# A windowed-attention and adapter kernel: fixed engine order, heads paired (n, n+4), fp32 hardware-queue loads, casts on GpSimd

## Chip, cores, metric

The kernel runs on one core of one Trainium2 chip. The metric is the device time of one execution in microseconds (us). Every run comes with a state: "slow" when it is over 1.5% above the fastest run of the same kernel. Ratios are the mean time of one kernel's fast runs over the mean of the other's fast runs of the same rounds on the same chip, so they are not quite the ratio of the medians quoted beside them.

Engines are named as in the profile: PE (matrix multiply), PEld (its weight loads), DVE (VectorE), ACT (ScalarE), POOL (GpSimd), SP (SyncE, which only issues transfers).

## The reference

```python
# q, k, v: (8 batches, 8 heads, 576 positions, 64), fp32
scores = q @ k.T / 8, masked to |i - j| <= 32; attn = softmax(scores); y = attn @ v
x = y as (8 * 576, 512)                      # all heads of a position side by side
logits = x @ w_gate                          # 8 experts, the best 2 are kept, softmax over these 2
out = x + sum over the 2 of weight * (x @ A[e]) @ B[e]     # A: 512 x 16, B: 16 x 512
```

## The kernel before

The work is cut into 32 units, each one pair of heads of one batch (four units a batch). A unit has nine blocks of 64 keys. Scores are made in tiles of eight blocks. The pieces:

```python
def load(b, w):                               # q or k: cast to fp16 during the transfer, issued by POOL
    for g in range(3): nc.gpsimd.dma_start(out=d[:, g]..., in_=src[g])
def load_v(b):                                # 16 small transfers a batch, also from POOL
    ...
def pair_heads(b, w):                         # DVE regroups q or k, 3 copies of 96x1024
    for g in range(3): nc.vector.tensor_copy(...)

def transposes(u, which):                     # tp: 6 PE transposes, then the copies to qT or kT
    ...
    if which == 0: nc.vector.tensor_copy(out=qTs[u % NQ]..., in_=tp...)
    else:          nc.vector.tensor_copy(out=kTs[u % NQ][0:64]...)      # half of kT by DVE
                   nc.scalar.copy(out=kTs[u % NQ][64:128]...)           # half by ACT
def score(t):                                 # ps: mask product, 8 score products, then exp on ACT
    ...
def pv(u):                                    # po: 13 products with v, then the softmax division:
    ...
    nc.vector.reciprocal(out=rc, in_=pog[:, :, :, D])
    nc.vector.tensor_tensor(out=xs[b]..., in0=pog[:, :, :, 0:D], in1=bcast(rc, 3, D), op=ALU.mult)
# ... moe_xT (tx), moe_zl (pz and the gate on DVE, then zs), moe_zT (tz), moe_out (pd), cut ...

for u in range(NU):                           # the loop (loads and pair_heads cut)
    if u + 2 < NU:
        transposes(u + 2, 0); transposes(u + 2, 1)
    if u + 1 < NU:
        scores_through(u + 1)                 # all tiles up to the end of unit u + 1
    pv(u)
    if u >= NP: moe_step(u - NP)              # a quarter of the adapter part of the batch before
```

In this kernel the source order is only a proposal: a scheduler reorders the instructions of each engine when it builds the program.

The softmax here doesn't subtract the row's maximum and nothing guards it: scores larger than these inputs give would overflow.

Of the kernel before, what the change touches and what calls it, by code (L numbers as in the profile page):

```python
# [28 lines left out]
def kernel(  # L29
# [27 lines left out]
    const = tc.alloc_tile_pool(name="const", bufs=1)  # L57
    load_pool = tc.alloc_tile_pool(name="load", bufs=2)
    cast_pool = tc.alloc_tile_pool(name="cast", bufs=2)
    x_pool = tc.alloc_tile_pool(name="xsb", bufs=2)  # L60
    moe_pool = tc.alloc_tile_pool(name="moe", bufs=2)
    ob_pool = tc.alloc_tile_pool(name="ob", bufs=3)
    small = tc.alloc_tile_pool(name="small", bufs=3)
    pw = tc.alloc_tile_pool(name="pw", bufs=3, space=bass.MemoryType.PSUM)
    pt = tc.alloc_tile_pool(name="pt", bufs=2, space=bass.MemoryType.PSUM)


    NV = 3
    vbd = [const.tile([128, NP, NB, 2 * VD], F16, name=f"vbd{i}") for i in range(NV)]

    def load(b, w):
        d = load_pool.tile([96, 3, H, 2, D], F16, tag=f"l{w}", name=f"l{w}")
        src = (q, k)[w][b].rearrange("h (g p j) d -> g p h (j d)", g=3, j=2)
        for g in range(3):
            nc.gpsimd.dma_start(
                out=d[:, g].rearrange("p h j d -> p h (j d)"), in_=src[g])
        raw[b, w] = d

    def load_v(b):
        d = vbd[b % NV]  # L80
        src = v[b].rearrange("(n h) (a p j) d -> h j n p a d", h=2, p=32, j=2)
        for n in range(NP):
            for h in range(2):
                for j in range(2):
                    p0 = 64 * h + 32 * j
                    nc.gpsimd.dma_start(  # L86
                        out=d[p0:p0 + 32, n, :, VD * h:VD * h + D], in_=src[h, j, n])

    def pair_heads(b, w):
        d = cast_pool.tile([96, 3, 2, H, D], F16, tag=f"c{w}", name=f"c{w}")  # L90
        for g in range(3):
            nc.vector.tensor_copy(out=d[:, g],
                                  in_=raw[b, w][:, g].rearrange("p h j d -> p j h d"))
        qk[b, w] = d

    raw, qk = {}, {}
    load(0, 0)
    load(0, 1)

    ident = const.tile([128, 128], F16)  # L100
    make_identity(nc, ident)

    for i in range(NV):
        nc.vector.memset(vbd[i], 0.0)
        nc.vector.memset(vbd[i][0:64, :, :, D], 1.0)
        nc.vector.memset(vbd[i][64:128, :, :, VD + D], 1.0)

    load_v(0)
    pair_heads(0, 0)
    pair_heads(0, 1)  # L110


    mask = const.tile([128, 4, 128], F16)
    nc.gpsimd.memset(mask, 0.0)
    for s in range(4):
        jk = s % 2
        blk = mask[32 * s:32 * s + 32]
        nc.gpsimd.affine_select(out=blk, in_=blk, compare_op=ALU.is_ge, fill=NEG,
                                base=-jk, channel_multiplier=-2,
                                pattern=[[0, 4], [1, 128]])  # L120
        nc.gpsimd.affine_select(out=blk, in_=blk, compare_op=ALU.is_ge, fill=NEG,  # L121
                                base=64 + jk, channel_multiplier=2,
                                pattern=[[0, 4], [-1, 128]])

    NQ = 4
    qTs = [const.tile([128, 2, 320], F16, name=f"qT{i}") for i in range(NQ)]
    kTs = [const.tile([128, NB, 128], F16, name=f"kT{i}") for i in range(NQ)]
    for t in qTs:
        nc.vector.memset(t[:, :, 0:16], 0.0)
        nc.vector.memset(t[:, :, 304:320], 0.0)  # L130
    for t in kTs:
        nc.vector.memset(t, 0.0)
    NPT = 4
    PTs = [const.tile([128, TB, 256], F16, name=f"PT{i}") for i in range(NPT)]
    for t in PTs:
        nc.vector.memset(t, 0.0)

    load(1, 0)
    load(1, 1)
    load_v(1)  # L140

    WA_sb = const.tile([128, 4, ER + E], F16)
    for c in range(4):
        nc.gpsimd.dma_start(
            out=WA_sb[:, c, 0:ER],
            in_=moe_A.transpose([1, 0, 2])[128 * c:128 * c + 128],
        )
    nc.gpsimd.dma_start(
        out=WA_sb[:, :, ER:],
        in_=moe_w_gate.rearrange("(c p) e -> p c e", p=128),  # L150
    )
    B_sb = const.tile([128, DD], F16)
    nc.gpsimd.dma_start(out=B_sb, in_=moe_B.rearrange("e r d -> (e r) d"))


    def transposes(u, which):
        b, n = divmod(u, NP)
        src = qk[b, which].rearrange("p g j h d -> p g j (h d)")
        tp = pt.tile([128, 1024], F16, tag="t", name="tp")
        for g in range(3):  # L160
            for j in range(2):
                if which == 0:
                    o = tp[:, 288 * j + 96 * g:288 * j + 96 * g + 96]
                else:
                    o = tp[:, 192 * g:192 * g + 192].rearrange(
                        "p (a j k) -> p a j k", a=3, j=2)[:, :, j]
                nc.tensor.matmul(  # L167
                    out=o, lhsT=src[:, g, j, 128 * n:128 * n + 128],
                    rhs=ident[0:96, 0:96], is_transpose=True, start=True, stop=True)
        if which == 0:  # L170
            nc.vector.tensor_copy(
                out=qTs[u % NQ][:, :, 16:304],
                in_=tp[:, 0:S].rearrange("p (j s) -> p j s", j=2))
        else:
            kt = tp[:, 0:S].rearrange("p (a k) -> p a k", k=64)
            nc.vector.tensor_copy(out=kTs[u % NQ][0:64, :, 0:64], in_=kt[0:64])  # L176
            nc.scalar.copy(out=kTs[u % NQ][64:128, :, 64:128], in_=kt[64:128])  # L177

# [17 lines left out]
    def pv(u):  # L196
# [4 lines left out]
        for g in range(NG):  # L201
# [11 lines left out]
        rc = small.tile([128, NG, 2], F32, tag="rc", name="rc")  # L213
        nc.vector.reciprocal(out=rc, in_=pog[:, :, :, D])  # L214
        nc.vector.tensor_tensor(  # L215
            out=xs[b][:, :, 128 * n:128 * n + 128].rearrange("p g (h d) -> p g h d", h=2),
            in0=pog[:, :, :, 0:D], in1=bcast(rc, 3, D), op=ALU.mult)


# [13 lines left out]
    def moe_zl(b):  # L233
        xT = st[b, "xT"]
        pz = pw.tile([128, 1024], F32, tag="w", name="pz")
        for g in range(NG):
            for c in range(4):
                nc.tensor.matmul(out=pz[:, GS * g:GS * g + ER + E],  # L238
                                 lhsT=xT[:, g, c, :], rhs=WA_sb[:, c, :],
                                 start=(c == 0), stop=(c == 3))  # L240
        pzg = pz[:, 0:GS * NG].rearrange("p (g c) -> p g c", c=GS)
        lg = pzg[:, :, ER:ER + E]

        def sm(name, shape):
            return small.tile([128, NG] + shape, F32, tag=name, name=name)
        m1, m2, dm, s = sm("m1", []), sm("m2", []), sm("dm", []), sm("s", [])
        is1, lm, is2, gate = sm("is1", [E]), sm("lm", [E]), sm("is2", [E]), sm("gate", [E])
        nc.vector.tensor_reduce(out=m1, in_=lg, axis=AX.X, op=ALU.max)
        nc.vector.tensor_tensor(out=is1, in0=lg, in1=bcast(m1, 2, E), op=ALU.is_ge)
        nc.vector.scalar_tensor_tensor(out=lm, in0=is1, scalar=-1e30, in1=lg,  # L250
                                       op0=ALU.mult, op1=ALU.add)
        nc.vector.tensor_reduce(out=m2, in_=lm, axis=AX.X, op=ALU.max)
        nc.vector.tensor_tensor(out=dm, in0=m2, in1=m1, op=ALU.subtract)
        nc.scalar.activation(out=dm, in_=dm, func=AF.Exp)
        nc.vector.tensor_tensor(out=is2, in0=lm, in1=bcast(m2, 2, E), op=ALU.is_ge)
        nc.vector.tensor_scalar(out=s, in0=dm, scalar1=1.0, scalar2=None, op0=ALU.add)
        nc.vector.reciprocal(out=s, in_=s)
        nc.vector.tensor_tensor(out=is2, in0=is2, in1=bcast(dm, 2, E), op=ALU.mult)
# [31 lines left out]
            r0 = S * b + 128 * g - 32  # L290
            nc.sync.dma_start(out=out[r0 + lo:r0 + hi], in_=ob[lo:hi, i])

    def moe_step(m):
        b, s = divmod(m, NP)
        if s == 0:
            for g in range(NG):
                moe_xT(b, g)
            moe_zl(b)
        elif s == 1:
            moe_zT(b)  # L300
            moe_out(b, [0, 1])
        elif s == 2:
            moe_out(b, [2, 3])
        else:
            moe_out(b, [4])


    for w in (0, 1):
        transposes(0, w)
    for w in (0, 1):  # L310
        transposes(1, w)
    t_done = 0

    def scores_through(u):
        nonlocal t_done
        last = min(NT - 1, (NB * u + NB - 1) // TB)
        while t_done <= last:
            score(t_done)
            t_done += 1

    scores_through(0)
    for u in range(NU):
        b, n = divmod(u, NP)
        if n == 0 and b + 1 < B:
            pair_heads(b + 1, 0)
        if n == 1 and b + 1 < B:
            pair_heads(b + 1, 1)
        if n == 0 and b + 2 < B:
            load(b + 2, 0)
            load(b + 2, 1)  # L330
            load_v(b + 2)
        if u + 2 < NU:
            transposes(u + 2, 0)
            transposes(u + 2, 1)
        if u + 1 < NU:
            scores_through(u + 1)
        pv(u)
        if u >= NP:
            moe_step(u - NP)
    for m in range(NU - NP, NU):  # L340
        moe_step(m)

    for p in (pt, pw, small, ob_pool, moe_pool, x_pool, cast_pool, load_pool, const):
        p.release()
# [30 lines left out]
```

## Time and profile before

| | before |
|---|---|
| time, median (range) | 216.44 us (215.23 to 217.51, 4 runs) |
| span of the profiled run | 211.4 us |
| fourth softmax division starts (batch 0 through the attention) | 44.4 us |
| from there to the last division, per batch (7 batches) | 21.35 us |
| last division to the end | 17.55 us |

The last three rows are read from the starts of the 32 reciprocals on DVE: 44.37 us for the fourth and 193.85 us for the last, (193.85 - 44.37) / 7 = 21.35.

The page of the profile: busy time of each engine with its share of the span; then, of the lines that cut the span into 40 slices, PEclk, the granted PE clock in tenths; then the chain of work that ended last, by engine.

```profile
PE 147.6 (70%) x1600; PEld 114.4 (54%) x1600; DVE 119.9 (57%) x337; ACT 85.6 (40%) x109; POOL 128.3 (61%) x197
...
PEclk9999999999969995999699997999999999999955
...
PE 52%; DVE 19%; POOL 11%; ACT 9%; issue 4%; DMA 3%; ACTq 0%; POOLq 0%
```

No engine is full. PE leads the chain, so what PE waits for counts. The view of waits for PE (waiting line, releaser, us in total, times, longest):

```profile
PE tz L271 <- DVE zs L262: 21.0, 8, 3.3
PE ps L182 <- POOL mask L121: 12.0, 1, 12.0
PE tp L167 <- POOL ident masks.py:199: 9.7, 1, 9.7
PE tx L227 <- DVE xT L230: 4.8, 6, 1.3
...
PE ps L186 <- ACT kT_164 L177: 2.4, 3, 1.3
```

PE stands still once per batch for the gate (zs), 21.0 us in all. Three windows round one gate wait (window, length, busy us and counts of PE, PEld, DVE, ACT, POOL; then granted clock, DMA share, GB/s):

```profile
98.00:101.90 3.90, 1.00 (x15) 0.75 (x13) 3.48 (x14) 1.75 (x3) 3.90 (x6) 1.00 0.73 46
102.20:106.20 4.00, 3.66 (x24) 1.97 (x22) 0.91 (x2) 1.76 (x3) 4.00 (x7) 0.57 1.03 75
106.80:112.00 5.20, 5.20 (x60) 4.25 (x57) 1.86 (x4) 3.90 (x5) 3.62 (x7) 1.00 1.46 177
```

Over the 4 us after the idle stretch the granted clock averages 0.57, so this PE wait is paid for twice.

### The profile page before, as it was taken

How to read it: one execution, taken by the hardware profiler on the slowest of the kernel's cores; microseconds unless marked ns; L12 is line 12 of the kernel's file. 1: busy time of each engine (PE TensorE's matmuls, PEld its weight loads, DVE VectorE, ACT ScalarE, POOL GpSimd, SP SyncE). 2: the span in 40 equal slices, each digit the busy share in tenths (PEclk: the TensorE clock that was granted, in tenths of full speed). 3: DMA queues.
4: the chain of work that ended last, by engine and by line, in shares of the span. 5: the costliest groups of instructions: out<-in, count | busy, mean ns of one | idle time of the engine just before them, and what ended most of it. 6: DMA issues, size and time to landing. Idle time of an engine off the chain costs nothing.

```text
span 211.4 us, 4124 instructions
## 1 busy us (share of the span) xinstructions
PE 147.6 (70%) x1600; PEld 114.4 (54%) x1600; DVE 119.9 (57%) x337; ACT 85.6 (40%) x109; POOL 128.3 (61%) x197
## 2 busy tenths in 40 slices
PE   0030279998299949987699729964998599848481
PEld 0010158996268835876378626864687468726330
DVE  6787026668814891379346851688349734844700
ACT  2001015663357334553275144723683466246032
POOL 7999995999799469835983797699480000000000
PEclk9999999999969995999699997999999999999955
DMA  6998099999999998998999999999993023003306
GB/s 59 157 63 56 1 140 125 67 42 154 138 101 144 244 96 54 208 210 87 63 167 249 103 89 153 258 98 147 172 189 55 0 90 136 5 0 123 100 0 223
DMA packets 86642, 24.12 MB, mean 114 GB/s; under 512 B 81888, under 2 KB 82016, under 8 KB 86624
## 3 DMA queue, kind: packets, MB, share of 16 engines
q0 software_dynamic: 81376, 14.44, 86.3%
q1 hardware_dynamic: 5248, 9.44, 13.2%
q8 instruction: 12, 0.20, 0.4%
q14 instruction: 6, 0.05, 0.1%
HBM read 28.85 MB, written 9.44 MB: 181 GB/s over the span
## 4 chain that ended last, share of the span: by engine, by line
PE 52%; DVE 19%; POOL 11%; ACT 9%; issue 4%; DMA 3%; ACTq 0%; POOLq 0%
PE ps L186 13%; PE po L206 9%; PE ps L182 7%; PE pd L282 5%; PE tp L167 5%; PE pd L284 5%; POOL vbd_82 L86 4%; DVE xb L215 4%; PE pz L238 3%; DMA l_189<-in_k_dram 3%; DVE zs L262 3%; PE tx L227 3%; DVE xT L230 3%; ACT zT L274 3%; PE tz L271 2%
## 5 line engine op out<-in xcount | busy, mean ns | idle before, releaser
L86 POOL DMA_DIRECT2D vbd_83<-in_v_dram x48 | 29.3, 616 | 12.0 <-DMA vbd_83<-in_v_dram 4.8
L86 POOL DMA_DIRECT2D vbd_82<-in_v_dram x48 | 29.3, 617 | 9.0 <-DMA l_496<-in_q_dram 2.7
L182 PE MATMUL ps<-mask,ident 128*128 128x512 f16 x72 | 24.6, 423 | 12.7 <-POOL mask L121 12.0
L214 DVE RECIPROCAL rc<-po 128x10 f32<-128x10 f32 x32 | 7.0, 218 | 38.2 <-PE po L206 38.1
L287 ACT COPY obt<-pd 128x1024 f32<-128x1024 f32 (+1 forms) x24 | 20.8, 869 | 16.8 <-PE pd L284 16.0
L215 DVE TENSOR_TENSOR xb<-po,rc 128x640 f16<-128x640 f32 x32 | 26.2, 820 | 0.7
L86 POOL DMA_DIRECT2D vbd_84<-in_v_dram x32 | 19.5, 619 | 7.3 <-DMA vbd_84<-in_v_dram 2.6
L282 PE MATMUL pd<-B_sb,zT 128*128 128x512 f16 x40 | 18.3, 459 | 4.2 <-ACT zT L274 4.2
L271 PE MATMUL tz<-ident,zs 128*128 128x128 f16 x40 | 4.0, 234 | 21.0 <-DVE zs L262 21.0
L227 PE MATMUL tx<-ident,xb 128*128 128x128 f16 x160 | 14.7, 220 | 5.4 <-DVE xT L230 4.8
L284 PE MATMUL pd<-xb,ident 128*128 128x512 f16 x40 | 18.4, 461 | 0.0
L230 DVE COPY xT<-tx 128x512 f16<-128x512 f16 x40 | 15.6, 416 | 2.4 <-PE tx L227 1.6
L177 ACT COPY kT_164<-tp 64x576 f16<-64x576 f16 x8 | 5.1, 633 | 25.0 <-DVE kT_164 L176 25.0
L227 PEld LDWEIGHTS <-xb 128*128 128x128 f16 x160 | 11.3, 101 | 6.9 <-issue 4.9
L271 PEld LDWEIGHTS <-zs 128*128 128x128 f16 x40 | 2.4, 102 | 22.8 <-DVE zs L262 22.8
L182 PEld LDWEIGHTS <-ident 128*128 128x128 f16 x72 | 6.6, 110 | 14.3 <-issue 14.1
L238 PE MATMUL pz<-WA_sb,xT 128*128 128x136 f16 x160 | 13.9, 223 | 0.4 <-DVE xT L230 0.4
L186 PE MATMUL ps<-qT_160,kT_164 128*128 128x128 f16 x72 | 11.1, 317 | 2.4 <-ACT kT_164 L177 2.4
L177 ACT COPY kT_161<-tp 64x576 f16<-64x576 f16 x8 | 5.1, 634 | 18.2 <-DVE kT_161 L176 18.1
L274 ACT COPY zT<-tz 128x640 f16<-128x640 f16 x8 | 5.5, 692 | 16.6 <-PE tz L271 16.6
L191 ACT ACTIVATE PT_178<-ps 128x1024 f16<-128x1024 f32 x9 | 9.2, 1023 | 6.6 <-PE ps L186 5.7
L191 ACT ACTIVATE PT_180<-ps 128x1024 f16<-128x1024 f32 x9 | 9.2, 1023 | 6.1 <-PE ps L186 5.2
(209 smaller groups left out, 375.4 us busy)
## 6 DMA issues: line engine op xcount, KB each, us to landing
out_dram<-obt SPq DMA_DIRECT2D x24, 256.0 KB, 4.0
out_dram<-obt SPq DMA_DIRECT2D x16, 192.0 KB, 2.7
vbd_82<-in_v_dram POOLq DMA_DIRECT2D x48, 36.0 KB, 2.8
vbd_83<-in_v_dram POOLq DMA_DIRECT2D x48, 36.0 KB, 3.4
vbd_84<-in_v_dram POOLq DMA_DIRECT2D x32, 36.0 KB, 3.2
l_85<-in_q_dram POOLq DMA_DIRECT2D x3, 192.0 KB, 4.8
l_89<-in_k_dram POOLq DMA_DIRECT2D x3, 192.0 KB, 6.4
l_185<-in_q_dram POOLq DMA_DIRECT2D x3, 192.0 KB, 4.6
```

The lines of the kernel that those rows point to most:

```text
L86: nc.gpsimd.dma_start(out=d[p0:p0 + 32, n, :, VD * h:VD * h + D], in_=src[h, j, n])
L182: nc.tensor.matmul(out=ps[:, i:i + 4], lhsT=ident, rhs=mask, start=True, stop=False)
L186: nc.tensor.matmul(out=ps[:, i].rearrange("p (k j) -> p j k", j=2), lhsT=kTs[u % NQ][:, a, :], rhs=qTs[u % NQ][:, :, 32 * a:32 * a + 64], ...
L191: nc.scalar.activation(out=PTs[t % NPT][:, :, 64:192], in_=ps, func=AF.Exp, scale=1.0 / float(D) ** 0.5)
L206: nc.tensor.matmul(out=po[:, GS * g:GS * g + 2 * VD], lhsT=PTs[t % NPT][:, sl, off:off + 128], rhs=vbd[b % NV][:, n, a, :], start=(i == 0) ...
L215: nc.vector.tensor_tensor(out=xs[b][:, :, 128 * n:128 * n + 128].rearrange("p g (h d) -> p g h d", h=2), in0=pog[:, :, :, 0:D], in1=bcast( ...
L227: nc.tensor.matmul(out=tp[:, 128 * c:128 * c + 128], lhsT=xs[b][:, g, 128 * c:128 * c + 128], rhs=ident, is_transpose=True, start=True, st ...
L230: nc.vector.tensor_copy(out=st[b, "xT"][:, g].rearrange("p c k -> p (c k)"), in_=tp[:, 0:512])
L238: nc.tensor.matmul(out=pz[:, GS * g:GS * g + ER + E], lhsT=xT[:, g, c, :], rhs=WA_sb[:, c, :], start=(c == 0), stop=(c == 3))
L282: nc.tensor.matmul(out=pd[:, i], lhsT=zT[:, g], rhs=B_sb, start=True, stop=False)
L284: nc.tensor.matmul(out=pd[:, i], lhsT=ident, rhs=xs[b][:, g], start=False, stop=True)
L287: nc.scalar.copy(out=ob[:, 0:n], in_=pd[:, 0:n])
```

## The change

The intent: free DVE of the regrouping and POOL of the issuing of 176 loads, load fp32 in few large transfers over the hardware queues, cast on POOL, which this leaves idle, pair heads (n, n+4), and lay the software pipeline by hand, so that the gate's latency is hidden. `manual_schedule` fixes each engine's order to the source order.

```diff
+    order = tc.manual_schedule()
+    ctx.enter_context(order)
...
+    def load_qk(b, w, eng, n0=0, n1=NP):      # fp32, issued by SP (first K by ACT)
+            for g in range(3): eng.dma_start(out=raw[b, w][:, g]..., in_=src[g])
+    def load_v(b, eng, n0=0, n1=NP):          # 4 transfers a batch instead of 16
+    def cast_qk(b, w, eng, n0=0, n1=NP):      # POOL: cast and regroup
+            eng.tensor_copy(out=qk[b, w][:, g, :, n0:n1]..., in_=raw[b, w][:, g, :, n0:n1]...)
+    def cast_v(b, eng, n0=0, n1=NP): ...
-    def pair_heads(b, w): ...
...
     for u in range(NU):
+        (loads of batch b + 2 on SP, casts of batch b + 1 on POOL)
         if u + 2 < NU:
             transposes(u + 2, 0)
             transposes(u + 2, 1)
+        last = min(NT - 1, (NB * min(u + 1, NU - 1) + NB - 1) // TB)
+        while done <= last:
+            score(done)
+            done += 1
+        if m >= 1 and n == 0: moe_out(m - 1, [2, 3])
+        if m >= 0 and n == 1: moe_zl(m)
+        if m >= 0 and n == 3: moe_zT(m)
         pv(u)
+        if m >= 0:
+            if n == 0: (five moe_xT)
+            elif n == 1: moe_gate(m, 0); moe_out(m - 1, [4])
+            elif n == 2: moe_gate(m, 1)
+            else:        moe_out(m, [0, 1])
```

More of the change, by code (lines that the diff above doesn't have):

```diff
@@ L59 @@
     cast_pool = tc.alloc_tile_pool(name="cast", bufs=2)
-    x_pool = tc.alloc_tile_pool(name="xsb", bufs=2)
+    x_pool = tc.alloc_tile_pool(name="xsb", bufs=3)
     moe_pool = tc.alloc_tile_pool(name="moe", bufs=2)
@@ L65 @@
     pt = tc.alloc_tile_pool(name="pt", bufs=2, space=bass.MemoryType.PSUM)
-    NV = 3
+    order = tc.manual_schedule()
+    ctx.enter_context(order)
+    NV = 2
     vbd = [const.tile([128, NP, NB, 2 * VD], F16, name=f"vbd{i}") for i in range(NV)]
-    def load(b, w):
-        d = load_pool.tile([96, 3, H, 2, D], F16, tag=f"l{w}", name=f"l{w}")
-        src = (q, k)[w][b].rearrange("h (g p j) d -> g p h (j d)", g=3, j=2)
-        for g in range(3):
-            nc.gpsimd.dma_start(
-                out=d[:, g].rearrange("p h j d -> p h (j d)"), in_=src[g])
-        raw[b, w] = d
@@ L79, in load_v @@
-    def load_v(b):
-        d = vbd[b % NV]
-        src = v[b].rearrange("(n h) (a p j) d -> h j n p a d", h=2, p=32, j=2)
-        for n in range(NP):
-            for h in range(2):
-                for j in range(2):
-                    p0 = 64 * h + 32 * j
-                    nc.gpsimd.dma_start(
-                        out=d[p0:p0 + 32, n, :, VD * h:VD * h + D], in_=src[h, j, n])
-    def pair_heads(b, w):
-        d = cast_pool.tile([96, 3, 2, H, D], F16, tag=f"c{w}", name=f"c{w}")
-        for g in range(3):
-            nc.vector.tensor_copy(out=d[:, g],
-                                  in_=raw[b, w][:, g].rearrange("p h j d -> p j h d"))
-        qk[b, w] = d
@@ L96, with raw_tiles @@
-    raw, qk = {}, {}
-    load(0, 0)
-    load(0, 1)
+    raw, qk = {}, {}
+    def raw_tiles(b):
+        for w in range(2):
+            raw[b, w] = load_pool.tile([96, 3, 2, NP, 2 * D], F32, tag=f"r{w}",
+                                       name=f"r{w}")
+            qk[b, w] = cast_pool.tile([96, 3, 2, NP, 2, D], F16, tag=f"c{w}",
+                                      name=f"c{w}")
+        raw[b, 2] = load_pool.tile([128, NP * NB, D], F32, tag="r2", name="r2")
+    def load_qk(b, w, eng, n0=0, n1=NP):
+        src = (q, k)[w][b]
+        if n1 - n0 == NP:
+            src = src.rearrange("h (g p j) d -> g p h (j d)", g=3, j=2)
+            for g in range(3):
+                eng.dma_start(out=raw[b, w][:, g].rearrange("p e n c -> p (e n) c"),
+                              in_=src[g])
+        else:
+            src = src.rearrange("(e n) (g p j) d -> e g p n (j d)", e=2, g=3, j=2)
+            for g in range(3):
+                for e in range(2):
+                    eng.dma_start(out=raw[b, w][:, g, e, n0:n1], in_=src[e, g][:, n0:n1])
@@ new lines, in load_v @@
+    def load_v(b, eng, n0=0, n1=NP):
+        src = v[b].rearrange("(e n) (a p j) d -> e j p (n a) d", e=2, p=32, j=2)
+        for e in range(2):
+            for j in range(2):
+                p0 = 64 * e + 32 * j
+                eng.dma_start(out=raw[b, 2][p0:p0 + 32, NB * n0:NB * n1],
+                              in_=src[e, j][:, NB * n0:NB * n1])
+    def cast_qk(b, w, eng, n0=0, n1=NP):
+        for g in range(3):
+            eng.tensor_copy(
+                out=qk[b, w][:, g, :, n0:n1].rearrange("p j n e d -> p e n j d"),
+                in_=raw[b, w][:, g, :, n0:n1].rearrange("p e n (j d) -> p e n j d", j=2))
@@ new lines, in cast_v @@
+    def cast_v(b, eng, n0=0, n1=NP):
+        dst = vbd[b % NV].rearrange("p n a c -> p (n a) c")
+        for e in range(2):
+            eng.tensor_copy(
+                out=dst[64 * e:64 * e + 64, NB * n0:NB * n1, VD * e:VD * e + D],
+                in_=raw[b, 2][64 * e:64 * e + 64, NB * n0:NB * n1])
+    NQ = 4
+    qTs = [const.tile([128, 2, 320], F16, name=f"qT{i}") for i in range(NQ)]
+    kTs = [const.tile([128, NB, 128], F16, name=f"kT{i}") for i in range(NQ)]
+    NPT = 4
+    PTs = [const.tile([128, TB, 256], F16, name=f"PT{i}") for i in range(NPT)]
@@ L100 @@
+    raw_tiles(0)
+    for n0 in (0, 2):
+        load_qk(0, 0, nc.sync, n0, n0 + 2)
+        load_qk(0, 1, nc.scalar, n0, n0 + 2)
+        load_v(0, nc.sync, n0, n0 + 2)
     ident = const.tile([128, 128], F16)
     make_identity(nc, ident)
-    for i in range(NV):
-        nc.vector.memset(vbd[i], 0.0)
-        nc.vector.memset(vbd[i][0:64, :, :, D], 1.0)
-        nc.vector.memset(vbd[i][64:128, :, :, VD + D], 1.0)
-    load_v(0)
-    pair_heads(0, 0)
-    pair_heads(0, 1)
     mask = const.tile([128, 4, 128], F16)
@@ L114 @@
     nc.gpsimd.memset(mask, 0.0)
-    for s in range(4):
-        jk = s % 2
-        blk = mask[32 * s:32 * s + 32]
+    for i in range(4):
+        jk = i % 2
+        blk = mask[32 * i:32 * i + 32]
         nc.gpsimd.affine_select(out=blk, in_=blk, compare_op=ALU.is_ge, fill=NEG,
@@ L123, with init_qkT, init_vbd, load_weights @@
                                 pattern=[[0, 4], [-1, 128]])
-    NQ = 4
-    qTs = [const.tile([128, 2, 320], F16, name=f"qT{i}") for i in range(NQ)]
-    kTs = [const.tile([128, NB, 128], F16, name=f"kT{i}") for i in range(NQ)]
-    for t in qTs:
-        nc.vector.memset(t[:, :, 0:16], 0.0)
-        nc.vector.memset(t[:, :, 304:320], 0.0)
-    for t in kTs:
-        nc.vector.memset(t, 0.0)
-    NPT = 4
-    PTs = [const.tile([128, TB, 256], F16, name=f"PT{i}") for i in range(NPT)]
-    for t in PTs:
-        nc.vector.memset(t, 0.0)
-    load(1, 0)
-    load(1, 1)
-    load_v(1)
-    WA_sb = const.tile([128, 4, ER + E], F16)
-    for c in range(4):
+    def init_qkT(i):
+        nc.vector.memset(qTs[i][:, :, 0:16], 0.0)
+        nc.vector.memset(qTs[i][:, :, 304:320], 0.0)
+        nc.vector.memset(kTs[i], 0.0)
+    def init_vbd(i):
+        nc.vector.memset(vbd[i], 0.0)
+        nc.vector.memset(vbd[i][0:64, :, :, D], 1.0)
+        nc.vector.memset(vbd[i][64:128, :, :, VD + D], 1.0)
+    init_qkT(0)
+    init_qkT(1)
+    nc.vector.memset(PTs[0], 0.0)
+    init_vbd(0)
+    nc.vector.memset(PTs[1], 0.0)
+    WA_sb = const.tile([128, 4, ER + E], F16)
+    B_sb = const.tile([128, DD], F16)
+    def load_weights():
+        for c in range(4):
+            nc.gpsimd.dma_start(
+                out=WA_sb[:, c, 0:ER],
+                in_=moe_A.transpose([1, 0, 2])[128 * c:128 * c + 128],
+            )
         nc.gpsimd.dma_start(
-            out=WA_sb[:, c, 0:ER],
-            in_=moe_A.transpose([1, 0, 2])[128 * c:128 * c + 128],
-        )
-    nc.gpsimd.dma_start(
-        out=WA_sb[:, :, ER:],
-        in_=moe_w_gate.rearrange("(c p) e -> p c e", p=128),
-    )
-    B_sb = const.tile([128, DD], F16)
-    nc.gpsimd.dma_start(out=B_sb, in_=moe_B.rearrange("e r d -> (e r) d"))
+            out=WA_sb[:, :, ER:],
+            in_=moe_w_gate.rearrange("(c p) e -> p c e", p=128),
+        )
+        nc.gpsimd.dma_start(out=B_sb, in_=moe_B.rearrange("e r d -> (e r) d"))
     def transposes(u, which):
         b, n = divmod(u, NP)
-        src = qk[b, which].rearrange("p g j h d -> p g j (h d)")
+        src = qk[b, which].rearrange("p g j n e d -> p g j n (e d)")
         tp = pt.tile([128, 1024], F16, tag="t", name="tp")
@@ L167, in transposes @@
                 nc.tensor.matmul(
-                    out=o, lhsT=src[:, g, j, 128 * n:128 * n + 128],
+                    out=o, lhsT=src[:, g, j, n],
                     rhs=ident[0:96, 0:96], is_transpose=True, start=True, stop=True)
@@ L215, in pv @@
         nc.vector.tensor_tensor(
-            out=xs[b][:, :, 128 * n:128 * n + 128].rearrange("p g (h d) -> p g h d", h=2),
+            out=xs[b].rearrange("p g (e n d) -> p g e n d", e=2, n=NP)[:, :, :, n],
             in0=pog[:, :, :, 0:D], in1=bcast(rc, 3, D), op=ALU.mult)
@@ L240, in moe_zl, with moe_gate @@
                                  start=(c == 0), stop=(c == 3))
+        st[b, "pz"] = pz
+    def moe_gate(b, part):
+        pz = st[b, "pz"]
         pzg = pz[:, 0:GS * NG].rearrange("p (g c) -> p g c", c=GS)
         lg = pzg[:, :, ER:ER + E]
-        def sm(name, shape):
-            return small.tile([128, NG] + shape, F32, tag=name, name=name)
-        m1, m2, dm, s = sm("m1", []), sm("m2", []), sm("dm", []), sm("s", [])
-        is1, lm, is2, gate = sm("is1", [E]), sm("lm", [E]), sm("is2", [E]), sm("gate", [E])
-        nc.vector.tensor_reduce(out=m1, in_=lg, axis=AX.X, op=ALU.max)
-        nc.vector.tensor_tensor(out=is1, in0=lg, in1=bcast(m1, 2, E), op=ALU.is_ge)
-        nc.vector.scalar_tensor_tensor(out=lm, in0=is1, scalar=-1e30, in1=lg,
-                                       op0=ALU.mult, op1=ALU.add)
-        nc.vector.tensor_reduce(out=m2, in_=lm, axis=AX.X, op=ALU.max)
-        nc.vector.tensor_tensor(out=dm, in0=m2, in1=m1, op=ALU.subtract)
-        nc.scalar.activation(out=dm, in_=dm, func=AF.Exp)
-        nc.vector.tensor_tensor(out=is2, in0=lm, in1=bcast(m2, 2, E), op=ALU.is_ge)
+        if part == 0:
+            for name, shape in (("m1", []), ("m2", []), ("dm", []), ("s", []),
+                                ("is1", [E]), ("lm", [E]), ("is2", [E]), ("gate", [E])):
+                st[b, name] = small.tile([128, NG] + shape, F32, tag=name, name=name)
+        m1, m2, dm, s, is1, lm, is2, gate = [
+            st[b, i] for i in ("m1", "m2", "dm", "s", "is1", "lm", "is2", "gate")]
+        if part == 0:
+            nc.vector.tensor_reduce(out=m1, in_=lg, axis=AX.X, op=ALU.max)
+            nc.vector.tensor_tensor(out=is1, in0=lg, in1=bcast(m1, 2, E), op=ALU.is_ge)
+            nc.vector.scalar_tensor_tensor(out=lm, in0=is1, scalar=-1e30, in1=lg,
+                                           op0=ALU.mult, op1=ALU.add)
+            nc.vector.tensor_reduce(out=m2, in_=lm, axis=AX.X, op=ALU.max)
+            nc.vector.tensor_tensor(out=dm, in0=m2, in1=m1, op=ALU.subtract)
+            nc.scalar.activation(out=dm, in_=dm, func=AF.Exp)
+            nc.vector.tensor_tensor(out=is2, in0=lm, in1=bcast(m2, 2, E), op=ALU.is_ge)
+            return
         nc.vector.tensor_scalar(out=s, in0=dm, scalar1=1.0, scalar2=None, op0=ALU.add)
@@ L291, in moe_out @@
             nc.sync.dma_start(out=out[r0 + lo:r0 + hi], in_=ob[lo:hi, i])
-    def moe_step(m):
-        b, s = divmod(m, NP)
-        if s == 0:
-            for g in range(NG):
-                moe_xT(b, g)
-            moe_zl(b)
-        elif s == 1:
-            moe_zT(b)
-            moe_out(b, [0, 1])
-        elif s == 2:
-            moe_out(b, [2, 3])
-        else:
-            moe_out(b, [4])
-    for w in (0, 1):
-        transposes(0, w)
-    for w in (0, 1):
-        transposes(1, w)
@@ L312 @@
-    t_done = 0
-    def scores_through(u):
-        nonlocal t_done
-        last = min(NT - 1, (NB * u + NB - 1) // TB)
-        while t_done <= last:
-            score(t_done)
-            t_done += 1
-    scores_through(0)
+    for n0 in (0, 2):
+        cast_qk(0, 0, nc.gpsimd, n0, n0 + 2)
+        cast_qk(0, 1, nc.vector, n0, n0 + 2)
+        cast_v(0, nc.gpsimd, n0, n0 + 2)
+        if n0 == 0:
+            for u in (0, 1):
+                transposes(u, 0)
+                transposes(u, 1)
+                if u == 0:
+                    score(0)
+                    nc.vector.memset(PTs[2], 0.0)
+                    nc.vector.memset(PTs[3], 0.0)
+            init_qkT(2)
+            init_qkT(3)
+            load_weights()
+            raw_tiles(1)
+            load_qk(1, 0, nc.sync)
+            load_qk(1, 1, nc.sync)
+            load_v(1, nc.sync)
@@ L322 @@
+    init_vbd(1)
+    done = 1
     for u in range(NU):
         b, n = divmod(u, NP)
-        if n == 0 and b + 1 < B:
-            pair_heads(b + 1, 0)
-        if n == 1 and b + 1 < B:
-            pair_heads(b + 1, 1)
+        m = b - 1
         if n == 0 and b + 2 < B:
-            load(b + 2, 0)
-            load(b + 2, 1)
-            load_v(b + 2)
+            raw_tiles(b + 2)
+            load_qk(b + 2, 0, nc.sync)
+            load_qk(b + 2, 1, nc.sync)
+        if n == 2 and b + 2 < B:
+            load_v(b + 2, nc.sync)
+        if b + 1 < B:
+            if n < 2:
+                cast_qk(b + 1, n, nc.gpsimd)
+            elif n == 2:
+                cast_v(b + 1, nc.gpsimd, 0, 2)
+            else:
+                cast_v(b + 1, nc.gpsimd, 2, 4)
@@ L332 @@
         if u + 2 < NU:
             transposes(u + 2, 0)
+        if u + 2 < NU:
             transposes(u + 2, 1)
-        if u + 1 < NU:
-            scores_through(u + 1)
-        pv(u)
-        if u >= NP:
-            moe_step(u - NP)
-    for m in range(NU - NP, NU):
-        moe_step(m)
+        last = min(NT - 1, (NB * min(u + 1, NU - 1) + NB - 1) // TB)
+        while done <= last:
+            score(done)
+            done += 1
+        if m >= 1 and n == 0:
+            moe_out(m - 1, [2, 3])
@@ new lines @@
+        if m >= 0 and n == 1:
+            moe_zl(m)
+        if m >= 0 and n == 3:
+            moe_zT(m)
+        pv(u)
+        if m >= 0:
+            if n == 0:
+                for g in range(NG):
+                    moe_xT(m, g)
+            elif n == 1:
+                moe_gate(m, 0)
+                if m >= 1:
+                    moe_out(m - 1, [4])
+            elif n == 2:
+                moe_gate(m, 1)
+            else:
+                moe_out(m, [0, 1])
+    m = B - 1
+    for g in range(NG):
+        moe_xT(m, g)
@@ L343 @@
+    moe_out(m - 1, [2, 3])
+    moe_zl(m)
+    moe_gate(m, 0)
+    moe_out(m - 1, [4])
+    moe_gate(m, 1)
+    moe_zT(m)
+    for gs in ([0, 1], [2, 3], [4]):
+        moe_out(m, gs)
     for p in (pt, pw, small, ob_pool, moe_pool, x_pool, cast_pool, load_pool, const):
```

## The prediction

> What bounds the kernel now. The chain that ended last is 52% PE, 19% DVE, 11% POOL, 9% ACT, 3% DMA. Three losses stand on it.
>
> (a) Start-up. In the order of time, POOL issues loads, then 16 small v loads (0.62 us each), then builds the mask; PE's first mask matmul waits for it until 24.9 us (12.0 us idle), the first probability-times-v matmul comes at 34.4 us.
>
> (b) A bubble per batch. In the waits, PE waits 21.0 us in 8 times for zs (the gate softmax). Afterwards 512-column matmuls start every 0.43 us, later every 0.215 us: half clock. The Trainium skill (TensorE: Matmul & The Clock Gate, "The HAM clock gate") says the PE halves its clock after an idle window of about 3.4 us; the trace agrees (granted-clock dips in the slices, 0.88 over batches at 58 to 103 us), though here already after 2.9 us of idle.
>
> (c) A tail of about 17 us after the last pv.
>
> Windows of 22 us show each batch: period 22.2 us, PE busy 17 to 19, DVE 12.5 to 14, ACT 10 to 11, POOL 16 to 20 (nearly all load issuing).
>
> At full clock, starts in the PE timeline give per batch: 48 transposes x 0.042, 9 masks x 0.215, 36 scores x 0.104, 52 pv x 0.06, 45 gating matmuls x 0.06, 10 output matmuls x 0.215, about 15.7 us. That is the floor the change can approach.
>
> The change. Removed: 48 DVE regroupings (20.3 us in all by the groups, 2.5 us a batch), one 2.0 us memset, 176 POOL load issues. Moved: gate, zT and output matmuls are staggered over units, so pv and scores lie between zs and tz; bubble (b) should vanish, about 2.6 us of wait plus about 2 us of half clock per batch. Added: POOL casts of 10,752 elements per partition per batch in 10 instructions. POOL's memset took 0.543 us for 512 elements and the affine select 0.63, about 1.0 to 1.2 ns per element; the Trainium skill (GPSIMD Engine Reference, 3.1) puts port-bound bodies at 1.03 cycles per element and a tight loop at 1.8. Estimate: 10.8 to 17 us a batch, off the chain while below the PE's period, but slower loads' casts delay the start. Loads keep 9,216 packets a batch, now unreduced. In 3 to 9 us the old q/k packets (512 B read) passed at about 24 ns per engine; all packets at that rate plus 3.5 us of stores give about 17 us a batch (estimate): close, probably hidden by two batches of prefetch.
>
> New stalls: the five xT copies (0.42 us) follow rc and xb (1.04 us) on DVE, with two transpose buffers, so PE loses about 2 us per batch; pz held across a unit costs about 0.5 us.
>
> Sum (estimates): batch 0 done near 36 us (POOL: mask to 10 us, casts, 5 us of weight issues, casts again, batch 1), then 7 batches x 18.3, then a tail of 16: span 180, time about 184 (runs exceed the span by 2 to 5 us).
>
> Range 168 to 208; faster by over 2%: 0.82, within 2%: 0.09, slower: 0.09.
>
> To check: PE's wait for zs falls under 5 us in total; clock stays near 1.0 between 40 us and the tail; period 17 to 19.5 us; first pv near 22 to 25 us; POOL copies of 1024 elements 0.95 to 1.6 us; DVE busy near 100 us; PE waits for xT copies remain.
>
> Wrong if: POOL casts cost over 1.8 ns per element (POOL then bounds at over 19 us a batch; at 2.2 ns about 240 us); 256- and 512-byte hardware-queue packets cost over 35 ns, or eight loads in flight are too few, so DMA bounds; or in-order engines expose waits that the old order hid.

## More of the kernel before

How the scheduler places the critical pieces is seen in the timeline (start, length, engine, line, operation; in brackets idle time of the engine before and what ended it):

```profile
112.97 0.42 PE L167 MATMUL tp<-ident,c_1299 96*128 96x96 f16 x6
113.23 0.60 PE L182 MATMUL ps<-mask,ident 128*128 128x512 f16 x2
113.48 0.45 DVE L171 COPY qT_159<-tp 128x576 f16<-128x576 f16 x1
...
113.67 0.38 PE L186 MATMUL ps<-qT_158,kT_162 128*128 128x128 f16 x2
113.84 0.90 PE L206 MATMUL po<-vbd_83,PT_179 128*128 128x130 f16 x12
113.85 0.44 DVE L176 COPY kT_163<-tp 64x576 f16<-64x576 f16 x1
114.32 0.63 ACT L177 COPY kT_163<-tp 64x576 f16<-64x576 f16 x1 [0.82 <-DVE kT_163 L176]
...
115.01 0.83 PE L186 MATMUL ps<-qT_159,kT_163 128*128 128x128 f16 x6
```

Here the scheduler has cut a score tile open: between its first blocks and those that need the new kT_163, PE runs the attention product po. The copies of kT finish meanwhile and PE does not wait. Nothing in the source says so.

## The result

The changed kernel is slower: 228.07 us median (227.60 to 228.51, 4 runs) against 216.44; ratio 1.054, 95% interval 1.048 to 1.060. The prediction had 184.

| | before | after | predicted |
|---|---|---|---|
| span | 211.4 | 225.8 | 180 |
| fourth division starts | 44.4 | 40.4 | 36 (batch 0 done) |
| per batch | 21.35 | 23.90 | 18.3 |
| last division to end | 17.55 | 18.1 | 16 |

After: (207.69 - 40.42) / 7 = 23.90. The start gained 4 us, the seven batches lost 7 x 2.55 = 17.9 us. The same lines of the page:

```profile
PE 152.1 (67%) x1600; PEld 115.3 (51%) x1600; DVE 112.3 (50%) x292; ACT 84.2 (37%) x109; POOL 95.8 (42%) x101
...
PEclk9995896999979999999999966999999988999996
...
PE 25%; DVE 23%; ACT 8%; issue 3%; ACTq 0%
```

DVE and POOL have less to do, as intended, and yet DVE's part of the chain has grown: 23 of the 59% that could be followed, against 19 of 98% before. (The shares of this page do not add to 100%: the chain could be followed back only part of the way.) PE's waits:

```profile
PE tp L187 <- POOL c_99 L105: 15.1, 6, 9.0
PE ps L206 <- ACT kT_91 L197: 13.6, 7, 3.8
PE tx L247 <- DVE xT L250: 9.2, 16, 1.1
PE tz L299 <- DVE zs L290: 5.7, 2, 2.9
PE ps L206 <- ACT kT_90 L197: 5.6, 5, 1.7
PE ps L206 <- ACT kT_92 L197: 3.8, 7, 1.0
PE pd L310 <- ACT zT L302: 3.0, 4, 0.8
PE ps L206 <- ACT kT_93 L197: 2.6, 4, 1.3
```

The gate wait did shrink, from 21.0 to 5.7 us. In its place stands a new one: scores wait for kT, 13.6 + 5.6 + 3.8 + 2.6 = 25.6 us against 2.4 + 0.4 = 2.8 before. From the waits of all engines:

```profile
DVE rc L234 <- PE po L226: 84.0, 30, 4.2
```

The head of DVE's queue is a softmax division that waits for PE, 84.0 us in all (before: 38.1), while PE waits for DVE's copies. One unit in the timeline shows the ring:

```profile
125.07 0.74 PE L226 MATMUL po<-vbd_84,PT_97 128*128 128x130 f16 x10
...
126.02 0.22 DVE L234 RECIPROCAL rc<-po 128x10 f32<-128x10 f32 x1 [3.41 <-PE po L226]
...
126.27 0.82 DVE L235 TENSOR_TENSOR xb<-po,rc 128x640 f16<-128x640 f32 x1
126.51 0.42 PE L187 MATMUL tp<-ident,c_1127 96*128 96x96 f16 x6
127.02 0.19 DVE L275 TENSOR_REDUCE m_1623<-pz 128x5 f32<-128x40 f32 x1
...
128.40 0.44 DVE L191 COPY qT_86<-tp 128x576 f16<-128x576 f16 x1
...
128.76 0.43 DVE L196 COPY kT_90<-tp 64x576 f16<-64x576 f16 x1
...
129.23 0.63 ACT L197 COPY kT_90<-tp 64x576 f16<-64x576 f16 x1 [0.16 <-DVE kT_90 L196]
...
129.92 0.99 PE L206 MATMUL ps<-qT_86,kT_90 128*128 128x128 f16 x4 [1.72 <-ACT kT_90 L197]
130.62 0.61 PE L226 MATMUL po<-vbd_84,PT_94 128*128 128x130 f16 x3
```

Read it from the top. Attention product of unit u on PE; its division on DVE, 1.04 us; the gate's small operations; only then, at 128.40, the copies of the transposes that PE had done by about 127; then ACT's half of kT; then the score blocks that reach into that unit; and behind those, in PE's fixed order, the next attention product. Reciprocal to reciprocal is one turn of this ring. The Trainium skill (TensorE: Matmul & The Clock Gate, the table at its head) says ACT and DVE take their queues strictly first in, first out, while PE only pulls weight loads ahead. The trace agrees: qT_86 could have been copied about 1.5 us earlier and was not.

### The profile page after: what moved, and what is told of

It reads as the page before. It is cut to its first block, busy times and chain, and to the rows that moved or that the text cites. A ratio compares the mean times of both kernels' runs of the same rounds, so it can differ in the third digit from the quotient of the medians.

```text
span 225.8 us, 4064 instructions
## 1 busy us (share of the span) xinstructions
PE 152.1 (67%) x1600; PEld 115.3 (51%) x1600; DVE 112.3 (50%) x292; ACT 84.2 (37%) x109; POOL 95.8 (42%) x101
## 4 chain that ended last, share of the span: by engine, by line
PE 25%; DVE 23%; ACT 8%; issue 3%; ACTq 0%
PE po L226 7%; DVE xb L235 6%; PE ps L206 4%; PE pd L310 3%; PE pz L258 3%; DVE xT L250 3%; PE pd L312 3%; PE tx L247 2%; DVE zs L290 2%; DVE rc L234 2%; PE tp L187 2%; ACT kT_93 L197 1%; ACT kT_92 L197 1%; ACT kT_91 L197 1%; ACT obt L315 1%
## 5 line engine op out<-in xcount | busy, mean ns | idle before, releaser
L202 PE MATMUL ps<-mask,ident 128*128 128x512 f16 x72 | 23.2, 405 | 3.0 <-DVE xb L235 1.9
L206 PE MATMUL ps<-qT_87,kT_91 128*128 128x128 f16 x72 | 12.2, 342 | 13.6 <-ACT kT_91 L197 13.6
L247 PE MATMUL tx<-ident,xb 128*128 128x128 f16 x160 | 13.8, 218 | 9.2 <-DVE xT L250 9.2
L310 PE MATMUL pd<-B_sb,zT 128*128 128x512 f16 x40 | 16.4, 409 | 3.0 <-ACT zT L302 3.0
L206 PEld LDWEIGHTS <-kT_91 128*128 128x128 f16 x72 | 7.9, 134 | 18.1 <-ACT kT_91 L197 15.9
L247 PEld LDWEIGHTS <-xb 128*128 128x128 f16 x160 | 10.2, 97 | 12.1 <-issue 11.1
L206 PE MATMUL ps<-qT_86,kT_90 128*128 128x128 f16 x72 | 12.1, 341 | 5.6 <-ACT kT_90 L197 5.6
L312 PE MATMUL pd<-xb,ident 128*128 128x512 f16 x40 | 15.7, 394 | 0.0
L206 PEld LDWEIGHTS <-kT_90 128*128 128x128 f16 x72 | 8.1, 136 | 10.3 <-ACT kT_90 L197 7.7
L187 PE MATMUL tp<-ident,c_99 96*128 96x96 f16 x24 | 3.0, 241 | 15.1 <-POOL c_99 L105 15.1
L206 PE MATMUL ps<-qT_88,kT_92 128*128 128x128 f16 x72 | 10.6, 306 | 3.8 <-ACT kT_92 L197 3.8
L206 PE MATMUL ps<-qT_89,kT_93 128*128 128x128 f16 x72 | 10.6, 306 | 2.9 <-ACT kT_93 L197 2.6
L211 ACT ACTIVATE PT_94<-ps 128x1024 f16<-128x1024 f32 x9 | 9.2, 1023 | 6.8 <-PE ps L206 6.8
L211 ACT ACTIVATE PT_95<-ps 128x1024 f16<-128x1024 f32 x9 | 9.2, 1023 | 5.7 <-PE ps L206 5.7
L258 PE MATMUL pz<-WA_sb,xT 128*128 128x136 f16 x160 | 11.1, 224 | 0.0
L211 ACT ACTIVATE PT_96<-ps 128x1024 f16<-128x1024 f32 x9 | 9.2, 1023 | 4.5 <-PE ps L206 4.4
```

The source lines that it names most:

```text
L202: nc.tensor.matmul(out=ps[:, i:i + 4], lhsT=ident, rhs=mask, start=True, stop=False)
L206: nc.tensor.matmul(out=ps[:, i].rearrange("p (k j) -> p j k", j=2), lhsT=kTs[u % NQ][:, a, :], rhs=qTs[u % NQ][:, :, 32 * a:32 * a + 64], ...
L211: nc.scalar.activation(out=PTs[t % NPT][:, :, 64:192], in_=ps, func=AF.Exp, scale=1.0 / float(D) ** 0.5)
L247: nc.tensor.matmul(out=tp[:, 128 * c:128 * c + 128], lhsT=xs[b][:, g, 128 * c:128 * c + 128], rhs=ident, is_transpose=True, start=True, st ...
L258: nc.tensor.matmul(out=pz[:, GS * g:GS * g + ER + E], lhsT=xT[:, g, c, :], rhs=WA_sb[:, c, :], start=(c == 0), stop=(c == 3))
L310: nc.tensor.matmul(out=pd[:, i], lhsT=zT[:, g], rhs=B_sb, start=True, stop=False)
```

## The experiments

Theory A: the hand order makes the loss, through this ring. Theory B (rival): the new loads and the GpSimd casts make it, by transfer rate, late landing or POOL's time. The experiments were run on three chips; each has its own runs of the kernel before beside it, and the ratios refer to those. The three time columns are in us, from the starts of the reciprocals in the profiled run as above.

| run | median us | ratio to before (95%) | 4th division | per batch | tail |
|---|---|---|---|---|---|
| changed kernel | 228.07 | 1.054 (1.048 to 1.060) | 40.4 | 23.90 | 18.1 |
| e1_sched | 209.84 | 0.975 (0.967 to 0.984) | slow profile | | |
| e2_ahead3 | 219.51 | 1.011 (0.999 to 1.023) | 41.2 | 22.19 | 19.6 |
| e4_noload (wrong result) | 222.49 | 1.027, see there | 40.6 | 22.96 | 18.1 |
| e6_oldload | 244.37 | 1.128 (1.115 to 1.140) | slow profile | | |
| e3_pvfirst | 202.38 | 0.933 (0.921 to 0.945) | 40.2 | 20.18 | 18.9 |
| e7_zTlate | 204.66 | 0.946 (0.936 to 0.955) | 41.0 | 20.45 | 19.0 |
| e8_xTact | 206.76 | 0.956 (0.941 to 0.971) | 39.9 | 20.65 | 20.0 |
| e9_wlate | 207.09 | 0.958 (0.948 to 0.968) | 37.8 | 20.97 | 20.8 |
| e10_pvfirst_zT | 194.53 | 0.903 (0.892 to 0.914) | 38.2 | 19.47 | 18.1 |
| e11_xTsplit | 197.96 | 0.921 (0.911 to 0.931) | 37.4 | 20.10 | 17.9 |
| e12_oldload_pvfirst | 213.16 | 0.985 (0.971 to 0.998) | 43.4 | 21.07 | 21.2 |
| e13_evaclate | 198.72 | 0.924 (0.916 to 0.933) | 39.7 | 19.79 | 18.0 |

All results but e4's were correct. Medians include slow runs, ratios do not.

### e1_sched: the order given back to the scheduler

```diff
-    order = tc.manual_schedule()
-    ctx.enter_context(order)
```

> The changed kernel with its hand order taken away (the two lines that fix each engine's order to program order; the scheduler orders the same instructions). Theory A (the hand order makes the loss: the score tile that reaches into the unit whose K was transposed just before it waits for DVE and ACT copies that stand behind the softmax division in DVE's queue): PE's waits for the ACT copy of kT, 25.6 us in all in the changed kernel, fall under 8 us, the period falls from 24.6 to under 22 us, time 195 to 212 us. Theory B (the new loads and GpSimd casts make the loss): time stays at 224 to 232 us.

Measured: ratio 0.975; the three fast runs took 209.28 to 210.25 us. The changed kernel's own loads and casts, under the scheduler, are faster than the kernel before. Its profile fell in the slow state, so its figures are not set against the others; in it PE waited 3.9 us for kT. Theory A held, B did not.

### e6_oldload: the old data path under the hand order

```diff
-    (SP and ACT loads, POOL casts, heads n and n+4)
+    (POOL loads that cast, three v buffers, DVE pair_heads, heads 2n and 2n+1, as before)
```

> The hand order of the changed kernel with the loads, the casts during the load and the DVE regrouping of the kernel before (heads paired as before). Theory A: it keeps the slow period, 25 to 28 us (DVE has 2.5 us a batch more in front of the kT copies) and needs 235 to 255 us. Theory B: the old loads repair it, 205 to 218 us.

Measured: ratio 1.128; fast runs 241.90 and 242.82 us. With e1 this closes a square: old path and scheduler 1, new path and scheduler 0.975, new path and hand order 1.054, old path and hand order 1.128. The hand order costs 8% (1.054 / 0.975) on the new path and 13% on the old; the new data path gains under either order. (e6 differs a little in the prologue, where the old loads issue.)

### e4_noload: loads and casts taken away after batch 1

```diff
-            raw_tiles(b + 2); load_qk(b + 2, 0, nc.sync); load_qk(b + 2, 1, nc.sync)
+            qk[b + 2, 0], qk[b + 2, 1] = qk[b, 0], qk[b, 1]     # old data, wrong result on purpose
-        if n == 2 and b + 2 < B: load_v(b + 2, nc.sync)
-        if b + 1 < B:
+        if b == 0:                                              # casts of batch 1 only
```

> Wrong result on purpose: the changed kernel without any load or cast after batch 1 (batches 0 and 1 are used again); PE, DVE and ACT keep their order. Theory A: the period stays at 24 to 25 us and time within 3 us of 228. Theory B (DMA rate, landing times or casts hold the steady state): time falls under 215 us.

Measured: the two fast runs took 221.29 and 219.85 us, the five fast ones of before 214.75 on average; 220.57 / 214.75 = 1.027. So neither expectation was met to the letter. Without any load or cast in the steady state the kernel is still slower than before, and PE still waits 23.9 us for kT; but some 2.6% (1.054 to 1.027) do hang on the loads and casts. PE's wait for kT in e4:

```profile
PE ps L206 <- ACT kT L197: 23.9, 23, 2.7
```

A candidate for part of these 2.6% is seen on DVE: five kinds of small gate operations whose inputs are both in SBUF (the on-chip memory beside the engines) took 11.87 us in all in the changed kernel and 7.34 us here, and they stand in front of the copies. The difference of two tiny vectors took 0.166 to 0.168 us in e4 in all eight cases, in the changed kernel up to 0.85 us. In e2_ahead3 one such operation is caught in the act:

```profile
100.35 2.03 POOL L105 CAST c<-r 96x1024 f16<-96x1024 f32 x2 [0.29 <-DMA r<-in_k_dram]
...
101.35 1.04 DVE L280 TENSOR_TENSOR dm<-m,m 128x5 f32<-128x5 f32 x1
```

The 5-element operation ends at 102.39 us, when the POOL casts end (102.38). The Trainium skill (GPSIMD Engine Reference, Specifications) says that GpSimd shares SBUF interfaces with VectorE and names instructions with two SBUF inputs as a case of contention; the trace agrees.

### e2_ahead3: the transposes one unit earlier

```diff
-        if u + 2 < NU: transposes(u + 2, 0)
-        if u + 2 < NU: transposes(u + 2, 1)
+        if u == 0: transposes(2, 0); transposes(2, 1)
+        if u + 3 < NU: transposes(u + 3, 0); transposes(u + 3, 1)
...
-            if n < 2: cast_qk(b + 1, n, nc.gpsimd)
+            if n == 0: cast_qk(b + 1, 0, nc.gpsimd); cast_qk(b + 1, 1, nc.gpsimd)
```

> The changed kernel with one thing moved: Q and K of a unit are transposed three units ahead instead of two (the four buffers allow it), the K casts following the Q casts directly. Theory A: the waits for kT fall from 25.6 us to under 5 us, the period to 20.5 to 22 us, time 200 to 210 us. Theory B: PE waits for the GpSimd casts instead, and time stays above 222 us.

Measured: 217.99 and 216.81 us in the fast runs, ratio 1.011. The kT waits are gone as expected, yet the time fell by 4% only, to 7 to 8 us above the range expected. PE's waits say where it went:

```profile
...
PE pd L310 <- ACT zT L302: 11.8, 7, 2.4
...
PE tz L299 <- DVE qT L191: 4.5, 4, 1.9
...
PE ps L206 <- ACT kT L197: 0.4, 1, 0.4
```

zT rose from 3.0 to 11.8 us, and tz now waits for qT as well. The wait for zT is not DVE's queue alone: at 85.57 us in this trace its copy starts on ACT only behind the exp of a score tile (1.02 us), and PE waits 1.47 us for it. Removing one wait handed most of its time on to others: the listed waits sum to 58.6 us against 67.5, though those for kT fell by 25.2, and the span is 9.6 us shorter at the same mean clock (0.939).

### e7_zTlate, e8_xTact, e9_wlate: one wait after the other, on top of e2

```diff
# e7: zT last in its batch, every moe_out one unit later
-        if m >= 0 and n == 3: moe_zT(m)
         pv(u)
+            (n == 3:) moe_zT(m)        # and moe_out(m - 1, ...) in n == 0, 1, 2
# e8: three of the five xT copies on ACT
+        if g % 2 == 0: nc.scalar.copy(out=dst, in_=tp[:, 0:512])
# e9: load_weights() after the casts of batch 1
```

> Transposes three units ahead as in e2_ahead3, and the transposed gate output taken apart: zT is made behind the attention product at the end of a batch, and all output products stand one unit later. Theory A2 (in e2_ahead3 the gain of the kT waits was handed on to the next in-order wait, PE for zT 11.8 us and for zs or qT 10.2 us): these fall under 3 us together and time is 8 to 14 us below e2_ahead3. If another stream (casts, loads) had taken the gain, time stays within 3 us of e2_ahead3.

> e7_zTlate with three of the five xT copies of a batch on ACT instead of DVE. The wait of PE for xT copies, 8.7 us in e2_ahead3, falls under 4 us; time 3 to 6 us below e7_zTlate. ACT, at about 10 us of 22 busy, should not become the bound.

> e8_xTact with the six weight loads (5.2 us of GpSimd issue) moved behind the casts of batch 1. PE's wait for the second half's Q cast, 5.1 us in the changed kernel, falls under 2 us; time 2 to 5 us below e8_xTact, and below both kernels of the case, 188 to 200 us.

Measured: e7 took 13 us less than e2's fast runs (0.946 against 1.011, on two chips), as expected; PE's wait of pd for zT fell to 0.8 us. The waits for zs and qT did not all go (2.6 us for zs; 3.4 us of the next transposes for qT), so the three stay above the 3 us expected. e8 and e9 missed: no gain, rather 2 us more than e7. In e8 PE waited 4.4 us for the xT copies of DVE and 6.0 us for those of ACT, where e7 had 9.1 us; only the engine waited for had changed. In e9 batch 0 was done 2 us sooner than in e8, and one wait of 5.2 us of the transposes was gone, but their wait for qT rose from 3.6 to 6.8 us and they waited another 2.6 for the first casts on DVE; the seven batches and the tail lost the rest, at a mean clock of 0.935 against 0.975. Why was not tested.

### e3_pvfirst: the attention product before the scores

```diff
             transposes(u + 2, 1)
+        pv(u)
         last = min(...)
         while done <= last: score(done) ...
...
         if m >= 0 and n == 3: moe_zT(m)
-        pv(u)
# and score(1) in the prologue
```

> The changed kernel with the attention product of a unit placed before the score tiles instead of behind them (two-ahead transposes kept; tile 1 is scored in the prologue). PE then has 0.8 us of work to cover the copies of qT and kT, and these stand before the division (1.04 us) in DVE's queue. Theory A: waits for kT fall from 25.6 us to under 8 us, time 208 to 219 us. If the kT waits were only a symptom of slow DVE or ACT copies as such, time stays above 224 us.

Measured: 200.19 to 202.62 us in the fast runs, ratio 0.933, better than expected. This is the order that the scheduler had made in the cut of the kernel before shown above. PE's waits, of which only the first two and the one for kT are shown:

```profile
PE tp L187 <- POOL c L105: 17.0, 9, 9.0
PE pd L310 <- ACT zT L302: 10.2, 8, 1.5
...
PE ps L206 <- ACT kT L197: 3.2, 6, 1.0
```

The kT waits fell from 25.6 to 3.2 us.

### e13_evaclate: PE's order untouched, two DVE instructions moved per unit

e3 changes two queues at once: PE gets cover, and the division moves behind the copies in DVE's queue. This run changes DVE's queue alone.

```diff
     pv(u):  (13 products)
-        nc.vector.reciprocal(...); nc.vector.tensor_tensor(...)
+    def pv_evac(u): nc.vector.reciprocal(...); nc.vector.tensor_tensor(...)
...
             transposes(u + 2, 1)
+        if u > 0: pv_evac(u - 1)
```

> The changed kernel, PE order untouched; on DVE alone the division of a unit (reciprocal and multiply, 1.04 us) is moved behind the next unit's qT and kT copies. Theory A: the loop PE product, DVE division, DVE copies, ACT copy, PE score gets about 1 us shorter in most units: waits for kT fall from 25.6 us to 5 to 15 us, time 207 to 220 us. If DVE's queue is not in the loop, time stays above 225 us.

Measured: 197.96 to 199.68 us, ratio 0.924; the expectation was met in the waits and surpassed in the time. PE's wait for kT here:

```profile
PE ps L206 <- ACT kT L197: 11.7, 20, 2.0
```

The place of two instructions in one queue makes the difference between 5.4% slower and 7.6% faster than before. The same place of the pipeline as shown for the changed kernel:

```profile
110.84 0.91 PE L227 MATMUL po<-vbd,PT 128*128 128x130 f16 x13
...
112.02 0.67 PE L187 MATMUL tp<-ident,c 96*128 96x96 f16 x12
...
112.48 0.46 DVE L191 COPY qT<-tp 128x576 f16<-128x576 f16 x1 [0.23 <-PE tp L187]
112.85 0.44 DVE L196 COPY kT<-tp 64x576 f16<-64x576 f16 x1
...
113.22 0.20 DVE L240 RECIPROCAL rc<-po 128x10 f32<-128x10 f32 x1
...
113.33 1.29 PE L206 MATMUL ps<-qT,kT 128*128 128x128 f16 x8
113.45 0.82 DVE L241 TENSOR_TENSOR xb<-po,rc 128x640 f16<-128x640 f32 x1
...
114.42 0.96 PE L227 MATMUL po<-vbd,PT 128*128 128x130 f16 x13
```

From product to product it is 3.58 us (110.84 to 114.42) where the changed kernel needed 5.55 (125.07 to 130.62). DVE copies qT 0.46 us after the transposes begin, and the gate's small operations, which no longer stand behind a division that waits for PE, are done by then. DVE's wait for the attention product fell from 84.0 to 0.5 us. Less contention with the POOL casts is not the reason: the five kinds of gate operations named under e4 took 13.17 us here, more than the 11.87 of the changed kernel.

PE's waits of over 0.2 us that the view lists sum to 67.5 us in the changed kernel and 44.9 here, 22.6 less. The granted clock rose from 0.939 to 0.965; the lost share, 0.061 x 225.8 against 0.035 x 196.2, is 6.9 us less (an estimate: it takes PE as busy while the clock is low). Together 29.5 us, and the spans differ by 29.6. The agreement is no separate proof, since one term is an estimate and not every wait need lengthen the span.

### e12_oldload_pvfirst, e10_pvfirst_zT, e11_xTsplit

e12 is e6 with the move of e3. e10 is e3 with the late zT of e7. e11 is e10 with the last two moe_xT in the next unit.

> e6_oldload (hand order, loads and DVE regrouping of the kernel before) with the attention product before the scores. Theory A: the fault of the hand order does not depend on the data path, so 242 us falls to 208 to 222 us, and the distance to e3_pvfirst, 8 to 18 us, is what the new loads and GpSimd casts are worth under a good order. If the new data path is needed for the repair, it stays above 230 us.

> e3_pvfirst with the output products one unit later and the transposed gate output last in its unit, as in e7_zTlate. The wait of PE for zT, 10.2 us in e3_pvfirst, falls under 2 us; time 5 to 10 us below e3_pvfirst, 190 to 198 us. If the wait is only handed on to another in-order wait, the gain is under 3 us.

> e10_pvfirst_zT with three of the five x transposes in the first unit of a batch and two in the second. PE's waits for xT copies, 4.9 us in e3_pvfirst, fall under 2.5 us; time 1 to 4 us below e10_pvfirst_zT, or no gain if the two scattered groups wait for the two transpose buffers instead.

Measured: e12 fell from ratio 1.128 to 0.985, so the repair does not need the new data path; e3 over e12 is 0.933 / 0.985, 5% for the new loads and casts under a good order (each ratio against the kernel before on its own chip). e10 met its expectation: 192.51 to 194.93 us, ratio 0.903, the best kernel. Its wait of pd for zT is 0.8 us, though 4.9 us of waits for zT turned up at the next transposes. e11 missed, 3.9 us more than e10 in the mean: the waits of tx for xT rose from 3.8 to 7.6 us, the second of the two outcomes that its expectation named.

## Why the prediction was wrong

Point by point:

- **What bounds before.** Right in kind: chain led by PE, a gate bubble per batch with half clock after it, a late start, a tail of 17.5 us. The bubble was removed as foreseen, 21.0 to 5.7 us (just over the 5 us named).
- **The step that failed**: "New stalls: the five xT copies (0.42 us) follow rc and xb (1.04 us) on DVE, with two transpose buffers, so PE loses about 2 us per batch; pz held across a unit costs about 0.5 us." The list was short by one. The score tile reaches into the unit whose transposes stand right in front of it, and its qT and kT copies stand behind the same rc and xb on DVE. I saw this queue for xT, once a batch, and not for qT and kT, which need it in every unit. It measured 25.6 us of kT waits, and it set the pace of the ring. The "7 batches x 18.3" was therefore 7 x 23.9: 39 of the 46 us by which the span was missed (180 against 225.8). e13 shows it: with DVE's order alone changed, 19.8 us a batch. The 1.5 us that are still missing to 18.3 were not taken apart.
- **Rooted in**: the floor of 15.7 us a batch, from PE's starts at full clock, plus stalls counted one by one. Such a sum holds only while the engines are decoupled. The one-line warning at the end ("in-order engines expose waits that the old order hid") named the cause, but was given less than a tenth of the odds.
- **Start.** The first attention product came at 25.4 us (predicted 22 to 25, before 34.4), but batch 0 was done at 40.4, not 36: of the 9 us gained, 4 were left at the end of batch 0. The wait for the casts of the second half (5.1 us, behind 5.2 us of weight issues) lies before the first attention product. After it, until 40.4, PE's listed waits are 1.8 us for a cast of batch 1, whose load came late, and 2.1 us for kT, and from 34.4 to 37.8 us the clock was 0.51; in the same stretch of the kernel before PE waited 0.4 us, at clock 1.00.
- **Casts.** Right: 1024 elements took 1.03 us on POOL, 1.0 ns per element, at the lower end of the 0.95 to 1.6 us predicted. The port-bound 1.03 cycles per element of the Trainium skill (GPSIMD Engine Reference, 3.1) would be 0.86 ns at its 1.2 GHz without any fixed cost (an estimate); the trace agrees, being somewhat longer. POOL was never the steady bound. DVE fell to 112.3 us busy, 12 more than predicted.
- **Loads.** Not the bound of the steady state, as predicted: e4 took them away and left most of the loss. The rival theory B is worth at most about 2.6%.
- **Clock.** Wrong: not near 1.0 in the steady state but 0.93 to 1.0 by batch, 0.96 over the seven batches (before: 0.94). In e13, where PE waited less, it was 1.00 over the same seven batches.
- **Tail.** 18.1 us against 16.

What stays open: how the 2.6% of e4 divide between DVE operations held by POOL casts and waits for data at the batch boundaries; I did not take that apart further.

## What to carry to other kernels

When an order is fixed by hand, walk once round every ring of engines (here PE product, DVE division, DVE copy, ACT copy, PE score) and put first in each in-order queue what another engine is waiting for, last what nobody needs soon: the division was needed only by the adapter part, one to four units later. A busy sum per engine does not see such a ring; a wait of the follower for the leader on both sides (DVE for PE 84 us, PE for DVE and ACT 25.6 us) does. If taking one wait away gives less than its total, look which wait took over before doubting the cause.

## What the Trainium skill lacked or had wrong

- GPSIMD Engine Reference, 3.1: no figure for a cast. Here 96x1024 fp32 to fp16 with regrouping took 1.03 us and 64x1152 took 1.16 us.
- TensorE: Matmul & The Clock Gate, "The HAM clock gate": it gives an idle window of about 3.4 us. Here the clock was 0.50 from 102.3 to 105.7 us of the kernel before, behind an idle stretch of 2.90 us; behind another, of 2.71 us, it was 1.00 (146 to 150 us).
- DMA: Bandwidth & Descriptors: it has no measured rate on this chip for hardware-queue loads in short runs. Here loads in runs of 256 and 512 bytes, nearly all on hardware queues and with no stores beside them, moved 213 GB/s over the first 34.6 us.
- No page says that a scheduler's order may hide a dependence that a hand order must then keep by itself; here that was 8 to 13% of the time.
